# Windowed attention and MLP on one core: masks as a bias in PSUM for row 0, a shared normalisation, and a different order of loads

## The chip, the cores and the metric

One core of a Trainium2 chip. The metric is the device time of one execution in microseconds (us), and times are medians over several executions. With one core there is no second die to compare with, but every execution carries its mean granted TensorE clock.

## The reference

```python
# q, k, v: (8, 8, 576, 64); w_in: (512, 2048); w_out: (2048, 512)
rel = pos[:, None] - pos[None, :]
mask_plain = (rel >= 0) & (rel < 32)                            # heads 0-3, "sliding"
mask_dil = (rel >= 0) & (rel < 128) & (rel % 4 == 0)            # heads 4-7, "dilated"
attn = softmax(where(mask, scale * q @ k.T, -1e9)) @ v          # per batch row and head
x = attn.transpose(0, 2, 1, 3).reshape(8 * 576, 512)
out = relu(x @ w_in) ** 2 @ w_out
```

(Softmax and MLP are shortened to one line each.) The kernel works by batch row, 0 to 7. The MLP of one row runs on TensorE while the attention of the next is prepared. Only row 0 has no MLP to hide behind, and the change is about row 0, plus one load in row 1.

## The kernel before

The parts touched, with cuts marked. Row 0 in program order; each engine executes its own instructions in this order.

```python
    def load_sliding_v(b):                        # v as fp32 into a staging tile
        vv = v[b, 0:HH].rearrange("h (m p) d -> p h m d", p=QB)
        if b == 0:
            for m in range(NB):                   # six transfers, one for each 96 tokens
                nc.sync.dma_start(out=sv[PADP:P, :, m, :], in_=vv[:, :, m, :])
        else: ...
    def halo_sliding(b, mp):                      # rows that reach into the block before
        m0, m1 = max(1, 2 * mp), 2 * mp + 2
        nc.scalar.copy(vp[b % 2][0:PADP, m0:m1, :, 0:D],
                       vp[b % 2][P - PADP : P, m0 - 1 : m1 - 1, :, 0:D])
    def fill_gen(): ...                           # filler: 2 matmuls of 512 columns, result unused
    def softmax(u, ps, mask):
        nc.scalar.activation(AT[:, u, 0:UW], ps[:, :, 0 : UW // 2], ACTF.Exp, scale=scale)
        nc.vector.tensor_mul(AT[:, u, 0:UW], AT[:, u, 0:UW], mask)
    def s_sliding(b, hp):
        tiles = [pa(f"ps{b}_{hp}_{half}") for half in range(2)]   # two PSUM tiles of two banks
        ...                                       # scores, start=True
        for half, ps in enumerate(tiles):
            softmax(2 * hp + half, ps, maskp)
    def normalize(b, what, pav, w):               # value product / sum of weights
        ...
        nc.vector.reciprocal(rcp[0:w], pv[:, :, :, D])
        nc.vector.tensor_tensor(out=x[0:w], in0=pv[:, :, :, 0:D], in1=rcp..., op=ALU.mult)
        return x
...
    load_sliding_v(0)
    load_dilated_v(0, nc.sync)
    cast_sliding_v(0, (0, 2))                     # fp32 -> fp16 on GpSimd
    load_w_in()                                   # three pieces, also issued by GpSimd
    cast_sliding_v(0, (4,))
    cast_dilated_v(0)
    for hp in range(2):
        t_sliding(0, n, hp, False)                # transposes of q and k
    pending.append(fill_gen())
    for hp in range(2):
        s_sliding(0, hp)
        pump(1)                                   # one filler round
    halo_sliding(0, 0)
    for a in range(2):
        t_dilated(0, m, a, False)
    halo_sliding(0, 1)
    pump(1)
    xs = [av_sliding(0, 0)]                       # first value product
    pump(1)
    for g in range(2):
        s_dilated(0, g)
        pump(1)
    halo_sliding(0, 2)
    ...
    load_v(1)
    cast_sliding_v(1)
    load_w_out((3,))
    cast_dilated_v(1)
    ...
    for mp in (1, 2):
        xs.append(av_sliding(0, mp))
        pump(1)
    ...                                           # x_sliding and av_dilated, with fillers
    zs = [av_dilated(0, 1, 0)]
    begun = [mm1_begin(0, 0)]
    zs.append(av_dilated(0, 1, 1))
    begun.append(mm1_begin(0, 1))
    x_dilated(0, 0, ys, False)
    x_dilated(0, 1, zs, False)                    # then TensorE's unbroken stream
```

The softmax here doesn't subtract the row's maximum and nothing guards it: scores larger than these inputs give would overflow.

## Time and profile before

| what | before |
|---|---|
| time, median (range), 3 runs | 310.51 us (309.01 to 310.66) |
| span of the profiled execution | 307.3 us |
| TensorE busy | 290.7 us, 95% |
| q and k of row 0 have landed | 6.62 us |
| first exponential of sliding / dilated scores starts | 8.69 / 14.70 us |
| third value product starts | 17.86 us |
| third reciprocal of the dilated heads starts | 22.23 us |
| TensorE's unbroken stream starts | 25.06 us |
| first 60 matmuls of the stream take | 13.11 us |

How to read it: after 25 us TensorE is busy nearly without a break, so the end of the program is the start of that stream plus its length. Whatever shortens row 0's chain moves the end; all else in row 0 is free. The profile's lines are in the prediction below.

### The profile page before, as it was taken

To read this page: it belongs to the slowest core of one execution; us is meant where nothing else is said; L and a number is where in the kernel's file an instruction comes from. 1 tells how busy PE (TensorE), PEld (TensorE's weight loads), DVE (VectorE), ACT (ScalarE), POOL (GpSimd) and SP (SyncE) were. 2 spreads that over 40 slices of the span, in tenths; PEclk is the share of its full clock that TensorE was granted. 3 is DMA by queue.
4 is the path that set the end of the run, shared out by engine and by line. 5 is a ranking of instruction groups with operands and counts; after the bars stand their busy time and mean duration, and the time that the engine had idled before them with its cause. 6 is when DMAs were issued, how large, how long until landed. Compare 5 with 4: busy or idle time off the path is not lost.

```text
span 307.3 us, 7108 instructions
## 1 busy us (share of the span) xinstructions
PE 290.7 (95%) x2874; PEld 196.5 (64%) x2874; DVE 207.9 (68%) x433; ACT 183.4 (60%) x326; POOL 71.7 (23%) x114
## 2 busy tenths in 40 slices
PE   1798998999999999999999999999999999999994
PEld 1454554554455469656998997569756975785583
DVE  7784448568953798489748983898378934834652
ACT  2766648668645982598339834983499336425620
POOL 4481008413805303400630083007000000000000
PEclk9999999999999999999999999999999999999999
DMA  7899997999699999999968996889500020003004
GB/s 116 188 200 213 206 171 114 189 241 205 112 214 194 222 199 185 240 154 191 171 130 188 181 184 97 219 166 186 165 10 2 0 109 29 0 4 136 2 0 137
DMA packets 67024, 43.58 MB, mean 142 GB/s; under 512 B 48624, under 2 KB 59376, under 8 KB 66992
## 3 DMA queue, kind: packets, MB, share of 16 engines
q1 hardware_dynamic: 57920, 28.45, 44.9%
q0 software_dynamic: 9072, 14.68, 27.7%
q8 instruction: 22, 0.36, 0.5%
q14 instruction: 10, 0.08, 0.1%
HBM read 36.70 MB, written 16.52 MB: 173 GB/s over the span
## 4 chain that ended last, share of the span: by engine, by line
PE 71%; ACT 10%; DVE 7%; DMA 6%; issue 2%; SPq 2%; POOL 1%; POOLq 0%; DVEq 0%
PE ph L294 27%; PE pa L371 16%; PE pb L371 8%; PE po L437 7%; ACT AT L547 5%; DMA ns<-in_q_dram 5%; PE pc L371 4%; ACT rt L317 3%; PE paw L619 3%; PE pav L605 2%; PE px L634 1%; PE py L652 1%; DVE AT L548 1%; DMA QKTp<-dp 1%; PE pf L491 1%
## 5 line engine op out<-in xcount | busy, mean ns | idle before, releaser
L294 PE MATMUL ph<-xT,wi 128*128 128x512 f16 (+1 forms) x640 | 133.4, 359 | 0.7 <-ACT xT L658 0.7
L317 ACT ACTIVATE rt<-ph 128x512 f16<-128x512 f32 x144 | 84.9, 603 | 33.5 <-PE ph L294 33.5
L294 PEld LDWEIGHTS <-wi 128*128 128x128 f16 x640 | 68.6, 114 | 46.8 <-issue 0.8
L318 DVE TENSOR_TENSOR g<-rt 128x512 f16<-128x512 f16 x144 | 62.2, 435 | 42.7 <-ACT rt L317 41.1
L371 PEld LDWEIGHTS <-g 128*128 128x128 f16 x448 | 42.5, 98 | 5.3
L170 POOL CAST vp<-sv 128x512 f16<-128x512 f32 x24 | 17.5, 760 | 108.6 <-DMA sv<-in_v_dram 62.1
L371 PEld LDWEIGHTS <-gs 128*128 128x128 f16 x336 | 31.6, 98 | 3.7 <-DVE gs L328 0.3
L437 PE MATMUL po<-wo,g 128*128 128x512 f16 x128 | 33.1, 379 | 0.0
L398 DVE TENSOR_TENSOR ov<-pb,ov 128x512 f32<-128x512 f32 x14 | 9.7, 691 | 29.9 <-PE pb L371 18.2
L371 PE MATMUL pa<-wt,gs 128*128 128x256 f16 x224 | 28.5, 273 | 0.0
L371 PE MATMUL pb<-wt,g 128*128 128x256 f16 x224 | 27.7, 273 | 0.0
L178 POOL CAST vd<-sd 128x512 f16<-128x512 f32 (+1 forms) x32 | 24.2, 782 | 3.1 <-DMA sd<-in_v_dram 2.4
L387 ACT COPY ov<-pa 128x512 f32<-128x512 f32 x14 | 8.2, 585 | 26.8 <-PE pa L371 26.8
L591 DVE TENSOR_TENSOR x_d<-paw,rcp_d 72x512 f16<-72x512 f32 x32 | 22.0, 687 | 1.1
L547 ACT ACTIVATE AT<-pz 128x576 f16<-128x576 f32 x32 | 20.0, 712 | 1.7 <-PE pz L576 1.6
L548 DVE TENSOR_TENSOR AT<-AT,maskp 128x576 f16<-128x576 f16 x32 | 17.3, 545 | 5.1 <-ACT AT L547 2.6
L547 ACT ACTIVATE AT<-ps 128x576 f16<-128x576 f32 x32 | 19.2, 662 | 1.2 <-PE ps L557 0.9
L658 ACT COPY xT<-py 128x576 f16<-128x576 f16 x16 | 10.2, 640 | 14.7 <-PE py L652 14.6
L591 DVE TENSOR_TENSOR x_p<-pav,rcp_p 96x512 f16<-96x512 f32 x24 | 16.5, 687 | 0.8
L387 ACT COPY ou<-pa 128x512 f32<-128x512 f32 x14 | 8.2, 588 | 14.5 <-PE pa L371 14.5
L548 DVE TENSOR_TENSOR AT<-AT,maskd 128x576 f16<-128x576 f16 x32 | 14.9, 484 | 2.6 <-ACT AT L547 0.6
L640 ACT COPY xT<-px 128x576 f16<-128x576 f16 x16 | 10.2, 638 | 9.2 <-PE px L634 8.6
(81 smaller groups left out, 306.6 us busy)
## 6 DMA issues: line engine op xcount, KB each, us to landing
sv<-in_v_dram SPq DMA_DIRECT2D x14, 288.0 KB, 6.2
dp<-nr SPq DMA_DIRECT2D x12, 288.0 KB, 4.1
out_dram<-ou SPq DMA_DIRECT2D x6, 512.0 KB, 3.1
out_dram<-ov SPq DMA_DIRECT2D x6, 512.0 KB, 3.5
sd<-in_v_dram SPq DMA_DIRECT2D x8, 320.0 KB, 7.3
ns<-in_k_dram POOLq DMA_DIRECT2D x8, 288.0 KB, 5.2
ns<-in_q_dram POOLq DMA_DIRECT2D x8, 288.0 KB, 6.4
sd<-in_v_dram SPq DMA_DIRECT2D x8, 256.0 KB, 6.7
```

The source lines that it names most:

```text
L170: nc.gpsimd.tensor_copy(vp[b % 2][:, m : m + 2, :, 0:D], sv[:, :, m : m + 2, :].rearrange("p h m d -> p m h d"))
L178: nc.gpsimd.tensor_copy(vd[b % 2][p0:P, t, c : c + 2, :, 0:D], sd[p0:P, t, :, D * c : D * (c + 2)].rearrange("p h (c d) -> p c h d", d=D),)
L294: nc.tensor.matmul(ph[:, t0:t1], wi4[ffc // 4][:, dmk, :, ffc % 4], xT[:, dmk, x0 : x0 + t1 - t0], start=(dmk == 0 and t0 == 0), stop=(dmk ...
L317: nc.scalar.activation(rt, ph[:], ACTF.Relu)
L318: nc.vector.tensor_mul(g[:, ffc, :], rt, rt)
L371: nc.tensor.matmul(banks[bank][:, t], a(k, t), b(k), start=(new and t == 0 and k == 0), stop=(k == HF - 1), skip_group_check=True,)
L387: nc.scalar.copy(ot, banks[A])
L437: nc.tensor.matmul(po, g[:, ffc, t * P : (t + 1) * P], wo[ffc // 4][:, ffc % 4, :], start=(ffc == 0), stop=(ffc == NFF - 1),)
L547: nc.scalar.activation(AT[:, u, 0:UW], ps[:, :, 0 : UW // 2], ACTF.Exp, scale=scale)
L548: nc.vector.tensor_mul(AT[:, u, 0:UW], AT[:, u, 0:UW], mask)
L591: nc.vector.tensor_tensor(out=x[0:w], in0=pv[:, :, :, 0:D], in1=rcp[0:w].unsqueeze(3).to_broadcast([w, 2, HH, D]), op=ALU.mult,)
L640: nc.scalar.copy(xT[:, 0:2, t0 : t0 + 288], px[:, 0:UW].rearrange("x (c t) -> x c t", c=2),)
```

## The change

Its intent, as far as the code tells: take VectorE out of row 0's chain. The masks are no longer multiplied in after the exponential; a bias of 0 or -30000 is put into the score tile by an identity matmul first, and the scores accumulate onto it. Sliding v comes in two transfers, so that SyncE issues less. GpSimd's casts stand between the pieces of w_in. Two of the dilated normalisations give half of their work to ScalarE. The sliding halo copies go to VectorE. Row 0's order is new: the first dilated scores come ahead of the first value product. Row 1: w_out's last quarter is issued ahead of the casts of v.

```diff
 def load_sliding_v(b):
-    if b == 0:
-        for m in range(NB):
-            nc.sync.dma_start(out=sv[PADP:P, :, m, :], in_=vv[:, :, m, :])
-    else: ...
+    for h in (0, 2):
+        nc.sync.dma_start(out=sv[PADP:P, h : h + 2], in_=vv[:, h : h + 2])
 def halo_sliding(b, mp):
-    nc.scalar.copy(
+    copy(nc.scalar if b else nc.vector,
+for o, m in ((biasp, maskp), (biasd, maskd)):
+    nc.vector.tensor_scalar(out=o, in0=m[:, 0 : UW // 2], scalar1=-1.0, scalar2=30000.0,
+                            op0=ALU.add, op1=ALU.mult)
 def softmax(u, ps, mask):
-    nc.vector.tensor_mul(AT[:, u, 0:UW], AT[:, u, 0:UW], mask)
+    if mask is not None: ...                      # row 0 has none
+def biased(b, ps, bias):
+    if b == 0:
+        for e in range(2):
+            nc.tensor.matmul(ps[:, e, 0 : UW // 2], ident, bias, start=True, stop=False, ...)
+    return ps
 def s_sliding(b, hp):                             # s_dilated likewise
-    tiles = [pa(f"ps{b}_{hp}_{half}") for half in range(2)]
+    tiles = [biased(b, pa(f"ps{b}_{hp}_{half}"), biasp) for half in range(2)]
 def normalize(b, what, pav, w, shared=False):     # shared: row 0, second dilated half
+    if shared:
+        for h in range(HH):
+            nc.scalar.activation(x[0:w, 1, h], pv[:, 1, h, 0:D], ACTF.Copy,
+                                 scale=rcp[0:w, 1, h : h + 1])
+    n = 1 if shared else 2                        # VectorE: n of 2 halves
 def x_dilated(b, t, xs, wide):                    # row 0, t = 1: copy split likewise
+        nc.scalar.copy(o[:, 0], i[:, 0])
+        nc.vector.tensor_copy(o[:, 1], i[:, 1])
 ...                                               # row 0
-    cast_sliding_v(0, (0, 2)); load_w_in(); cast_sliding_v(0, (4,)); cast_dilated_v(0)
+    cast_sliding_v(0, (0,)); load_w_in(0); cast_sliding_v(0, (2, 4))
+    cast_dilated_v(0, (0,)); load_w_in(1); cast_dilated_v(0, (1,)); load_w_in(2)
     for hp in range(2):
         s_sliding(0, hp)
-        pump(1)
-    halo_sliding(0, 0)
     for a in range(2):
         t_dilated(0, m, a, False)
-    halo_sliding(0, 1)
     pump(1)
+    s_dilated(0, 0)
+    pump(1)
+    halo_sliding(0, 0)
     xs = [av_sliding(0, 0)]
     pump(1)
-    for g in range(2):
-        s_dilated(0, g)
-        pump(1)
-    halo_sliding(0, 2)
+    s_dilated(0, 1)
+    pump(1)
+    halo_sliding(0, 1)
 ...
-    cast_sliding_v(1)
+    nc.gpsimd.tensor_copy(seen, sv[:, 3, NB - 1, 0:1])   # row 1's sliding v has landed
     load_w_out((3,))
-    cast_dilated_v(1)
+    cast_v(1)
 ...
     for mp in (1, 2):
         xs.append(av_sliding(0, mp))
+        if mp == 1:
+            halo_sliding(0, 2)
         pump(1)
```

(x_dilated(0, 0) and the second mm1_begin change places; the small copies that hold v back until q has landed move from VectorE to GpSimd.)

More of the change, by code (lines that the diff above doesn't have):

```diff
@@ L95 @@
     maskd = const.tile([P, UW], FP16, name="maskd")
+    biasp = const.tile([P, UW // 2], FP16, name="biasp")
+    biasd = const.tile([P, UW // 2], FP16, name="biasd")
     def load_qk(b):
@@ L125, in load_sliding_v @@
         vv = v[b, 0:HH].rearrange("h (m p) d -> p h m d", p=QB)
-        if b == 0:
-            for m in range(NB):
-                nc.sync.dma_start(out=sv[PADP:P, :, m, :], in_=vv[:, :, m, :])
-        else:
-            for h in (0, 2):
-                nc.sync.dma_start(out=sv[PADP:P, h : h + 2], in_=vv[:, h : h + 2])
+        for h in (0, 2):
+            nc.sync.dma_start(out=sv[PADP:P, h : h + 2], in_=vv[:, h : h + 2])
     def load_dilated_v(b, eng):
@@ L142, in load_v, with load_w_in @@
         load_dilated_v(b, nc.sync)
-    def load_w_in():
-        f0 = 0
-        for t, w in zip(wi, wi_cols):
-            nc.gpsimd.dma_start(
-                out=t, in_=moe_w_in[:, f0 : f0 + w].rearrange("(dh dl) f -> dl dh f", dl=P)
-            )
-            f0 += w
+    def load_w_in(n):
+        f0, w = sum(wi_cols[:n]), wi_cols[n]
+        nc.gpsimd.dma_start(
+            out=wi[n], in_=moe_w_in[:, f0 : f0 + w].rearrange("(dh dl) f -> dl dh f", dl=P)
+        )
     def load_w_out(gs):
@@ L172, in cast_sliding_v, with cast_dilated_v @@
             )
-    def cast_dilated_v(b):
-        for t in range(2):
+    def cast_dilated_v(b, ts=(0, 1)):
+        for t in ts:
             p0 = 64 * t
@@ L184, in halo_sliding @@
         m0, m1 = max(1, 2 * mp), 2 * mp + 2
-        nc.scalar.copy(
-            vp[b % 2][0:PADP, m0:m1, :, 0:D], vp[b % 2][P - PADP : P, m0 - 1 : m1 - 1, :, 0:D]
+        copy(
+            nc.scalar if b else nc.vector,
+            vp[b % 2][0:PADP, m0:m1, :, 0:D],
+            vp[b % 2][P - PADP : P, m0 - 1 : m1 - 1, :, 0:D],
         )
@@ L271 @@
             hi_[:, 0:w].unsqueeze(1).to_broadcast([P, m.shape[1], w]),
+        )
+    for o, m in ((biasp, maskp), (biasd, maskd)):
+        nc.vector.tensor_scalar(
+            out=o, in0=m[:, 0 : UW // 2], scalar1=-1.0, scalar2=30000.0, op0=ALU.add, op1=ALU.mult
         )
@@ L547, in softmax @@
         nc.scalar.activation(AT[:, u, 0:UW], ps[:, :, 0 : UW // 2], ACTF.Exp, scale=scale)
-        nc.vector.tensor_mul(AT[:, u, 0:UW], AT[:, u, 0:UW], mask)
+        if mask is not None:
+            nc.vector.tensor_mul(AT[:, u, 0:UW], AT[:, u, 0:UW], mask)
+    def biased(b, ps, bias):
+        if b == 0:
+            for e in range(2):
+                nc.tensor.matmul(
+                    ps[:, e, 0 : UW // 2], ident, bias, start=True, stop=False, skip_group_check=True
+                )
+        return ps
     def s_sliding(b, hp):
-        tiles = [pa(f"ps{b}_{hp}_{half}") for half in range(2)]
+        tiles = [biased(b, pa(f"ps{b}_{hp}_{half}"), biasp) for half in range(2)]
         for half, ps in enumerate(tiles):
@@ L560, in s_sliding @@
                         QKTp[b % 2][r, 0, hp, PADP + QB * m : PADP + QB * (m + 1)],
-                        start=True,
+                        start=b > 0,
                         stop=True,
+                        skip_group_check=b == 0,
                     )
         for half, ps in enumerate(tiles):
-            softmax(2 * hp + half, ps, maskp)
+            softmax(2 * hp + half, ps, maskp if b else None)
     def s_dilated(b, g):
-        tiles = [pa(f"pz{b}_{g}_{h}") for h in range(2)]
+        tiles = [biased(b, pa(f"pz{b}_{g}_{h}"), biasd) for h in range(2)]
         for h, ps in enumerate(tiles):
@@ L579, in s_dilated, with normalize @@
                             QKTd[b % 2][r, 0, a, q0 : q0 + QD],
-                            start=True,
+                            start=b > 0,
                             stop=True,
+                            skip_group_check=b == 0,
                         )
         for h, ps in enumerate(tiles):
-            softmax(4 + 2 * g + h, ps, maskd)
-    def normalize(b, what, pav, w):
+            softmax(4 + 2 * g + h, ps, maskd if b else None)
+    def normalize(b, what, pav, w, shared=False):
         x = xp.tile([QB, 2, HH, D], FP16, name=f"x{b}_{what}", tag="x")
@@ L590, in normalize @@
         nc.vector.reciprocal(rcp[0:w], pv[:, :, :, D])
+        if shared:
+            for h in range(HH):
+                nc.scalar.activation(
+                    x[0:w, 1, h], pv[:, 1, h, 0:D], ACTF.Copy, scale=rcp[0:w, 1, h : h + 1]
+                )
+        n = 1 if shared else 2
         nc.vector.tensor_tensor(
-            out=x[0:w],
-            in0=pv[:, :, :, 0:D],
-            in1=rcp[0:w].unsqueeze(3).to_broadcast([w, 2, HH, D]),
+            out=x[0:w, 0:n],
+            in0=pv[:, 0:n, :, 0:D],
+            in1=rcp[0:w, 0:n].unsqueeze(3).to_broadcast([w, n, HH, D]),
             op=ALU.mult,
@@ L625, in av_dilated @@
                 )
-        return normalize(b, f"d{t}_{a}", pav, QD)
+        return normalize(b, f"d{t}_{a}", pav, QD, b == 0 and t == 1)
     def x_sliding(b, half, xs, wide):
@@ L657, in x_dilated @@
         t0 = (b * S + 288 * t) % XW
-        nc.scalar.copy(
-            xT[:, 2:4, t0 : t0 + 288].rearrange("x c (i r) -> x c i r", r=DIL),
-            py[:, 0:UW].rearrange("x (c r i) -> x c i r", c=2, r=DIL),
-        )
+        o = xT[:, 2:4, t0 : t0 + 288].rearrange("x c (i r) -> x c i r", r=DIL)
+        i = py[:, 0:UW].rearrange("x (c r i) -> x c i r", c=2, r=DIL)
+        if b == 0 and t == 1:
+            nc.scalar.copy(o[:, 0], i[:, 0])
+            nc.vector.tensor_copy(o[:, 1], i[:, 1])
+        else:
+            nc.scalar.copy(o, i)
     def attn_scores(b, gap, less=0, hooks={}):
@@ L706 @@
     n, m = nsd[0]
-    nc.vector.tensor_copy(sv[64:P, 0, :, 0], n[0:64, 0, 0:NB])
+    nc.gpsimd.tensor_copy(sv[PADP:64, :, 0, 0], n[PADP:64, :, 0])
     load_sliding_v(0)
-    nc.vector.tensor_copy(sd[64:P, :, 0, 0], n[0:64, 0, 0:2])
+    nc.gpsimd.tensor_copy(sd[64:P, :, 0, 0], n[64:P, 0, 0:2])
     load_dilated_v(0, nc.sync)
-    cast_sliding_v(0, (0, 2))
-    load_w_in()
-    cast_sliding_v(0, (4,))
-    cast_dilated_v(0)
+    cast_sliding_v(0, (0,))
+    load_w_in(0)
+    cast_sliding_v(0, (2, 4))
+    cast_dilated_v(0, (0,))
+    load_w_in(1)
+    cast_dilated_v(0, (1,))
+    load_w_in(2)
     for hp in range(2):
@@ L759 @@
     zs.append(av_dilated(0, 1, 1))
+    x_dilated(0, 0, ys, False)
     begun.append(mm1_begin(0, 1))
-    x_dilated(0, 0, ys, False)
     x_dilated(0, 1, zs, False)
```

## The prediction

> **What bounds the kernel now.** I read the page first (engine shares, slices), then a table by stage, then the chain in order of time for the first 30 us, then the timeline of each engine there, then the waits after 25 us.
>
> ```profile
> PE 290.7 (95%) x2874; PEld 196.5 (64%) x2874; DVE 207.9 (68%) x433; ACT 183.4 (60%) x326; POOL 71.7 (23%) x114
> 20.00:25.00 5.00, 3.58 (x54) 2.31 (x53) 3.38 (x8) 1.90 (x3) 3.76 (x7) 1.00 1.15 212
> 25.00:38.00 13.00, 12.94 (x60) 6.76 (x60) 6.02 (x15) 8.86 (x16) 0.54 (x2) 1.00 1.11 209
> 100.00:307.00 207.00, 202.28 (x1971) 149.38 (x1969) 141.54 (x284) 120.94 (x220) 32.44 (x48) 1.00 0.60 123
> ```
>
> The first line is the page; the others are stages (window, its length, busy time and count of PE, PEld, DVE, ACT, POOL, then clock, DMA share, GB/s). From 25 us on TensorE is 97 to 99% busy: only what moves the moment at which its unbroken stream starts, or a wait inside the stream, can move the end. The change touches row 0's attention, which is all of the first 25 us, so its worth is the shift of that moment. The chain in order of time (start, length, what) shows how it is reached:
>
> ```profile
> 16.13 1.20 ACT AT L547 x2
> 17.35 0.77 DVE AT L548
> 18.28 0.70 DVE x_p L591
> ...
> 22.45 0.69 DVE x_d L591
> 23.29 0.70 DVE x_d L591
> 24.03 0.32 PE py L652 x4
> 24.37 0.65 ACT xT L658
> 25.06 13.11 PE ph L294 x60
> ```
>
> From the last mask product at 17.35 to 23.98 it is VectorE with its six normalisations and short round trips to TensorE; then four transposes, one ScalarE copy, and the stream. Upstream, from the timelines:
>
> ```profile
> 8.82 1.04 PE L491 MATMUL pf<-maskp,ident 128*128 128x512 f16 x2
> 10.38 0.61 PE L491 MATMUL pf<-maskp,ident 128*128 128x512 f16 x2
> 16.04 2.09 DVE L548 TENSOR_TENSOR AT<-AT,maskd 128x576 f16<-128x576 f16 x3 [0.20 <-ACT AT L547]
> 17.21 2.63 POOL L178 CAST vd<-sd 128x512 f16<-128x512 f32 x4 [0.81 <-DMA sd<-in_v_dram]
> 7.34 3.96 SPq L128 DMA_DIRECT2D sv<-in_v_dram  x6
> 12.89 2.31 POOL L147 DMA_DIRECT2D wi<-in_moe_w_in_dram  x3
> ```
>
> Six v issues take 3.96 us of SyncE; the third sliding cast waits until 15.78, the dilated ones until 17.21. In the stream itself one wait is of interest, from the list of waits between 40 and 110 us:
>
> ```profile
> PE ps L557 <- DMA QKTp<-dp: 0.5, 1, 0.5
> ```
>
> It stands at 71.5 us (0.64 us beyond the matmul's own columns) and ends a chain of transfers for row 2.
>
> **What the Trainium skill says.** (1) "VectorE: DVE Perf Modes", The perf-mode tier table: a two-input 16-bit product from SBUF runs at 2x, anything from PSUM in fp32 at 1x. The trace agrees: the 576-wide mask product takes 0.46 us undisturbed, a 512-wide normalisation from PSUM 0.69. (2) "SBUF — State Buffer", Who interferes with whom: a VectorE instruction with two SBUF inputs contends with a GpSimd one that reads SBUF. It agrees: the same product takes 0.86 us at 11.48 and 0.77 at 17.35, both beside a GpSimd cast. (3) "ScalarE: Activation LUTs", What ACT_TABLE_LOAD costs: an activation costs 186 ns + 0.833 ns per element, a per-partition scale adds 93 ns, neighbours overlap by 93 ns. The first half agrees (666 ns for 576 wide; the exponentials take 650); the kernel before has no per-partition scale, so that part is untested. (4) "TensorE: Matmul & The Clock Gate", What's actually happening: half clock until some 3.4 us of activity. It agrees: the two filler matmuls at 8.9 us need 0.97 us on the chain, those at 10.4 need 0.43, and the clock record turns at 10.3.
>
> **The change part by part.** I replay row 0 in the new program order with durations of this trace.
>
> Fence and v load: the small copies that hold v back leave VectorE (where they stood behind the masks until 7.38) for GpSimd, free when q lands at 6.62. v issues at about 6.9 instead of 7.34, in two pieces instead of six. But until 9.5 us the engines are full with q and k, and the whole sliding v (590 KB) then needs about 2.8 us at 200 to 227 GB/s, so it lands near 12.3; the first cast now needs all of it: 12.9 instead of 12.03. Third cast 14.9 (was 16.39), dilated v cast by 16.1 and 18.1 (were 18.60 and 19.84). w_in's first piece is issued near 12.9 as before; being alone it lands near 18.5 (20.0 before), the others 1 to 2 us earlier. None of this is on the chain above: w_in is first needed at 21.4, and its last piece has some 3.5 us to spare.
>
> Bias, sliding: 16 identity matmuls of 288 columns, in groups of four. The first four start when the transposes end (7.65) at half clock: 4 x 0.24 = 0.96 us, against a wait for the q/k copies that ended at 8.23. So scores start near 8.65, 0.4 us late, exponentials near 9.1 (8.69 before). The second four wait for the score tiles that the exponentials free (9.75 and 10.3); those exponentials end near 12.1 instead of 11.45. The mask products (0.46 + 0.86 at the end) disappear; they ended at 12.34. Gain on this leg: about 0.2 us.
>
> Dilated q/k: ScalarE no longer stops for the first halo (12.06 to 12.46), VectorE is free at 11.3. Ready near 13.4 instead of 13.80.
>
> Middle: now the dilated scores of the first group come first. Exponential 13.85 to 14.5; the first value product needs that tile's bank, so its normalisation ends near 15.9 instead of 14.95; the second group's bias needs the bank which that frees: scores 16.2, exponentials 16.6 to 17.8 (before: 16.13 to 17.32, then masks to 18.13). Second value product 17.3, normalised at 18.64 (18.96 before). Then a step that was not there: the last sliding halo now queues on VectorE behind that normalisation, about 0.25 us, so the third value product starts near 18.95 instead of 17.86.
>
> Tail: from the third value product to the second dilated one TensorE does 0.25 + 4 fillers of 0.43 + two transposes of 0.26 + 0.25 = 2.7 us in order, so it is at 21.7 instead of 20.93, and its normalisation ends at 23.1 instead of 22.30. Sharing: four 64-wide ScalarE scalings at about 0.21 (0.165 fixed + 0.053 + 0.093 - 0.10, an estimate from the ScalarE page and this trace) make 0.94 us against 0.69 for VectorE's whole one; two in a row are 1.8 us of ScalarE, then the first copy 0.55, then half a copy 0.40: 2.7 us from the third reciprocal, against 2.59 measured before (22.42 to 25.01). Sharing is even. The stream starts between 25.5 and 26.1, 0.4 to 1.0 us LATER.
>
> w_out's last quarter: issued when row 1's sliding v has landed (45.2) instead of after its casts (47.01). The DMA engines stood idle from 46.8 to 48.7, so it lands nearly 2 us earlier, and row 2's loads behind it (landing at 54.6 to 59.2) about 1 us earlier; the wait of 0.64 us at 71.5 goes. Sum: +0.7 - 0.6 = about 0, from a before whose three runs lie at 309.0, 310.5 and 310.7 (mean 310.1).
>
> I then lean 0.4 us to the fast side, as my replay puts late several steps that hang on a bank coming free, and whoever arranged the order presumably saw a gain: 309.7.
>
> **Rivals.** (a) VectorE was the true limit and is relieved: eight products (4.96 us of VectorE in row 0), half of two normalisations and two fence copies go. For it: VectorE is busy nearly without a break from 15.4 to 20. Then the stream starts near 23.5 and the time is about 308.3. Against it: the two-tile ring of score banks sets the order of the middle. (b) Latency takes the place of throughput, as in my replay, with no relief at 71.5: 311. (c) The clock stays at half longer: two filler rounds at 8.8 and 10.4 are gone, and only 16 x 288 columns come in; cold dilated transposes would cost 1 us more: 311 to 312. (d) The transfers hide everything: the stream's loads have 3 us or more to spare, so even a start 2 us earlier would not meet them.
>
> **Range and chances.** Start of the stream -1.6 to +1.6 us, relief at 71.5 0 to -0.6, the spread between runs about 0.8 either way: 307.6 to 311.6. A move of 2% is 6.2 us, a quarter of all that precedes the stream; faster by that much 0.02, slower 0.01, within 0.97.
>
> **What would show it.** Right: the first bias matmuls near 7.7 us at about 0.24 us each; no mask product in row 0; first dilated exponential near 13.8; the third value product waiting for the VectorE halo and starting after 18.5; ScalarE's small scalings at 0.2 us apiece ending last before the copies; w_in's first piece landing before 19; no wait for the transposed q/k near 71 us; stream start 25 to 26.2. Wrong: a stream that starts before 24.5 (rival a), cold fillers after 11 us (rival c), or a new wait inside the stream for w_in, w_out or row 1's v.

## More of the kernel before

One line more for later, the row "TensorE's granted clock in tenths" of the page of the kernel before, in 40 slices. (The clock's record begins where it first turns to full, here at 10.30 us, so the half clock before that doesn't show in the row.)

```profile
PEclk9999999999999999999999999999999999999999
```

## The result, and the profile after

| | before | after |
|---|---|---|
| time, median (range), 4 runs each | 310.59 us (309.01 to 311.16) | 315.18 us (315.05 to 315.32) |
| span of the profiled execution | 307.3 us | 313.5 us |
| q and k landed | 6.62 | 7.14 |
| third sliding / first dilated exponential starts | 10.26 / 14.70 | 12.09 / 15.52 |
| third value product starts | 17.86 | 20.92 |
| third reciprocal of the dilated heads starts | 22.23 | 24.98 |
| stream starts | 25.06 | 29.06 |
| first 60 matmuls of the stream take | 13.11 | 15.89 |

The kernel after takes 1.56% longer: ratio 1.0156, 95% interval 1.0119 to 1.0193. A ratio is the mean time of one kernel's fast runs over that of the other's of the same rounds, so it is not quite the ratio of the medians quoted. That is within the 2% that the prediction put at 0.97, but the time lies 5.5 us above its number and well above its range.

The page of the kernel after: VectorE has the work taken from it that the change meant to take (207.9 to 202.6 us), and TensorE is busy *longer*; the row of its clock says why in part.

```profile
PE 296.2 (94%) x2886; PEld 198.9 (63%) x2886; DVE 202.6 (65%) x429; ACT 183.7 (59%) x331; POOL 70.5 (22%) x117
...
PEclk9997799999999999999999999999999999999999
```

The table by stage of the kernel after (columns as in the prediction: window, length, busy time of PE, PEld, DVE, ACT, POOL, clock, DMA share, GB/s) has the same two stages that were shown of before. From 25 to 38 us TensorE did 55 matmuls in place of 60 and the clock stood at 0.74:

```profile
20.00:25.00 5.00, 3.87 (x54) 2.44 (x54) 3.44 (x9) 2.00 (x4) 4.18 (x8) 1.00 1.11 182
25.00:38.00 13.00, 10.77 (x55) 4.80 (x56) 4.29 (x13) 6.94 (x17) 0.34 (x2) 0.74 1.12 208
```

The chain in order of time of the kernel after (start, length, what), cut to its three delays (pieces named "issue", of 0.05 us at most, are left out too):

```profile
8.35 1.07 PE ps L556 x4
9.42 0.37 PE ps L568 x5
9.82 0.66 ACT AT L549
10.52 1.18 PE ps L556 x4
11.70 0.60 PE ps L568 x12
12.29 2.02 PE pd L539 x18
...
20.48 0.39 DVE vp L162
20.92 0.43 PE pav L624 x8
...
25.21 0.93 ACT x_d L606 x4
26.16 0.42 DVE x_d L610
26.58 0.12 DVE rcp_d L603
26.73 0.93 ACT x_d L606 x4
27.68 0.43 DVE x_d L610
28.15 0.44 PE py L671 x4
28.61 0.41 ACT xT L680
29.06 15.89 PE ph L296 x60
```

First block: the bias matmuls (L556) and the 18 dilated transposes (L539) stand on the chain one after the other, both rounds of bias at half clock (the clock record turns full at 14.17 us; before, at 10.30). Second: the third value product waits for a halo copy on VectorE. Third: from the third reciprocal (24.98) to the stream it takes 4.1 us, before 2.8, because ScalarE's four small scalings and VectorE's half of the same normalisation run **in turn**, not side by side. VectorE's own timeline of the kernel after says it outright (in brackets: idle time before, and what ended it):

```profile
26.16 0.42 DVE L610 TENSOR_TENSOR x_d<-paw,rcp_d 72x256 f16<-72x256 f32 x1 [0.98 <-ACT x_d L606]
...
27.68 0.42 DVE L610 TENSOR_TENSOR x_d<-paw,rcp_d 72x256 f16<-72x256 f32 x1 [0.98 <-ACT x_d L606]
29.04 0.46 DVE L681 COPY xT<-py 128x288 f16<-128x288 f16 x1 [0.95 <-ACT xT L680]
```

The last line is the split copy: its two halves ran in turn as well.

Inside the stream, the list of TensorE's waits from 40 to 110 us of the kernel after no longer has a wait for the transposed q and k (QKTp), as predicted:

```profile
PE pav L624 <- ACT vp L160: 0.5, 1, 0.5
PE pz L588 <- ACT AT L549: 0.2, 1, 0.2
PE pav L624 <- DVE rcp_p L603: 0.2, 1, 0.2
```

So the span's 6.2 us are: stream start +4.0, its first 60 matmuls +2.8, the wait at row 2 -0.6. The difference of the medians is smaller (4.6) mainly because the profiled execution of before is a quick one (309.11 us against a median of 310.59), while that of after lies near its median (315.32 against 315.18). It has two spells of half clock in the stream and the other three runs of after have one each, yet all four lie within 0.27 us; what makes up for the second spell isn't known.

### The profile page after: what moved, and what is told of

Read it like the earlier page. It is cut to its first block, busy times and chain, and to the rows that moved or that the text cites.

```text
span 313.5 us, 7131 instructions
## 1 busy us (share of the span) xinstructions
PE 296.2 (94%) x2886; PEld 198.9 (63%) x2886; DVE 202.6 (65%) x429; ACT 183.7 (59%) x331; POOL 70.5 (22%) x117
## 4 chain that ended last, share of the span: by engine, by line
PE 76%; ACT 12%; DVE 6%; issue 3%; DMA 2%; POOL 0%; DVEq 0%; POOLq 0%
PE ph L296 30%; PE pa L373 15%; PE pb L373 8%; PE po L439 7%; ACT AT L549 7%; PE pc L373 4%; ACT rt L319 4%; PE paw L638 3%; PE pav L624 2%; DVE AT L551 2%; DMA ns<-in_q_dram 2%; PE py L671 1%; PE px L653 1%; DVE g L320 1%; PE pd L539 1%
## 5 line engine op out<-in xcount | busy, mean ns | idle before, releaser
L296 PE MATMUL ph<-xT,wi 128*128 128x512 f16 (+1 forms) x640 | 136.2, 364 | 0.5 <-ACT xT L680 0.5
L320 DVE TENSOR_TENSOR g<-rt 128x512 f16<-128x512 f16 x144 | 61.5, 430 | 44.9 <-ACT rt L319 43.6
L373 PEld LDWEIGHTS <-g 128*128 128x128 f16 x448 | 42.5, 98 | 5.3
L610 DVE TENSOR_TENSOR x_d<-paw,rcp_d 72x512 f16<-72x512 f32 (+1 forms) x32 | 21.4, 670 | 3.0 <-ACT x_d L606 2.0
L174 POOL CAST vd<-sd 128x512 f16<-128x512 f32 (+1 forms) x32 | 22.7, 736 | 0.6 <-DMA sd<-in_v_dram 0.2
L683 ACT COPY xT<-py 128x576 f16<-128x576 f16 x15 | 9.6, 641 | 12.3 <-PE py L671 12.3
L551 DVE TENSOR_TENSOR AT<-AT,maskp 128x576 f16<-128x576 f16 x28 | 13.6, 487 | 3.9 <-ACT AT L549 1.6
L439 PEld LDWEIGHTS <-g 128*128 128x128 f16 x128 | 10.3, 98 | 8.3 <-DVE g L320 0.3
```

The source lines that it names most:

```text
L174: nc.gpsimd.tensor_copy(vd[b % 2][p0:P, t, c : c + 2, :, 0:D], sd[p0:P, t, :, D * c : D * (c + 2)].rearrange("p h (c d) -> p c h d", d=D),)
L296: nc.tensor.matmul(ph[:, t0:t1], wi4[ffc // 4][:, dmk, :, ffc % 4], xT[:, dmk, x0 : x0 + t1 - t0], start=(dmk == 0 and t0 == 0), stop=(dmk ...
L320: nc.vector.tensor_mul(g[:, ffc, :], rt, rt)
L373: nc.tensor.matmul(banks[bank][:, t], a(k, t), b(k), start=(new and t == 0 and k == 0), stop=(k == HF - 1), skip_group_check=True,)
L439: nc.tensor.matmul(po, g[:, ffc, t * P : (t + 1) * P], wo[ffc // 4][:, ffc % 4, :], start=(ffc == 0), stop=(ffc == NFF - 1),)
L610: nc.vector.tensor_tensor(out=x[0:w, 0:n], in0=pv[:, 0:n, :, 0:D], in1=rcp[0:w, 0:n].unsqueeze(3).to_broadcast([w, n, HH, D]), op=ALU.mult,)
```

## The experiments

Eighteen kernels were run; the kernel before ran along on the same chip. Where the text compares traces it takes "stream minus q", the time from q's landing to the start of the stream, because q lands anywhere from 6.5 to 7.7 us in any of the kernels: 18.4 us before, 21.9 after. Two runs with row 0 as before and its tail untouched (b_wout 17.5) or filled (e_tail 18.5) show that this number too carries about 1 us of noise. A ratio is always against the kernel before. Waits of TensorE in the text count from the end of the columns of the matmul before; the lists of waits model a later end and give 0.1 to 0.2 us less.

**Spells of half clock.** In all 20 traces each stretch at half clock that lies between two at full clock is 3.41 us long or twice that. So an execution's mean granted clock tells how many such windows it had: one takes 0.5 x 3.41 / 310 = 0.0055 off the mean. 15 of 55 runs of the kernel before had a mean below 0.996; those average 311.98 us (311.84 without the one that is slow), the other 40 310.22. So a spell costs about 1.7 us, which is also half of 3.41, and the kernel before has one in a quarter of its executions. The counts for the others stand with each experiment.

### The four direct suspects

`a_unshared` (the kernel after, both shared steps undone):

```diff
-        return normalize(b, f"d{t}_{a}", pav, QD, b == 0 and t == 1)
+        return normalize(b, f"d{t}_{a}", pav, QD)
-        if b == 0 and t == 1:                     # split copy of xT
+        if False:
```

> The changed kernel without the sharing: row 0's normalisations and its last copy are whole again, on one engine each. Theory S (sharing serialises: in the changed kernel's trace VectorE's half waits 0.98 us for ScalarE's four scalings, twice, and the second half copy waits for the first): from the third dilated reciprocal to the stream 2.6 us as in the kernel before instead of 3.9, so the stream starts about 1.2 us earlier; if the busier tail also keeps TensorE's clock up, 1.7 to 3.4 us more. In all 311 to 314 us against 315.2. Rival (sharing is even, the loss is upstream in the bias and the order): 315 us within 0.3.

Measured: 313.25 us (311.97 to 314.32), ratio 1.0081 [1.0040, 1.0121]. From the third reciprocal to the stream 2.8 us again, the profiled run without a spell, 2 of 6 runs with one. About half of the loss hangs on the sharing (ratio 1.0081 in place of 1.0156), through the chain and through the clock.

`b_share` (the kernel before with the sharing and the split copy alone).

> The kernel before with the sharing alone added. Theory S: the stream starts about 1.2 us later (26.3), time +1.2 us; +3 to +4.6 if the longer quiet tail also drops the clock. Rival (sharing is even): within 0.3 us of the kernel before.

Measured: 311.82 us (311.14 to 313.79), ratio 1.0048 [1.0007, 1.0088]. The third reciprocal comes at 22.63, the stream at 26.59: 3.96 us, where before has 2.83. The same wait, on VectorE's timeline of this run, and the table by stage with half clock at the start of the stream:

```profile
23.80 0.42 DVE L597 TENSOR_TENSOR x_d<-paw,rcp_d 72x256 f16<-72x256 f32 x1 [0.98 <-ACT x_d L593]
...
25.32 0.42 DVE L597 TENSOR_TENSOR x_d<-paw,rcp_d 72x256 f16<-72x256 f32 x1 [0.98 <-ACT x_d L593]
```

```profile
25.00:38.00 13.00, 11.60 (x48) 5.51 (x49) 5.13 (x12) 7.79 (x15) 0.49 (x2) 0.87 1.11 210
```

5 of 6 runs had a spell. The sharing alone is therefore slower, though it moves work off the busy engine: both engines read the same PSUM tile, and in the built program VectorE's half waits on ScalarE's semaphore. Builds, without a run on the chip, tell what orders them: with an output tile for each engine the wait stays, with a tile of reciprocals for each it stays, and with a PSUM tile for each it is gone. So it is the read of the PSUM tile that is ordered. The Trainium skill, "PSUM — Partial Sum Buffer", PSUM bank collisions raise a hardware error, says that two engines on one bank must be kept apart, but that accesses to different banks run clean. The two halves lie in different banks of one tile, so by that page the order isn't needed; two PSUM tiles would be the way to get rid of it. That was not run. The split copy waits likewise (VectorE 0.83 us for ScalarE in this run), but its tile is a single bank, 1024 fp16 elements per partition, so there the order is needed.

`a_warm` (the kernel after, nine filler matmuls around the last transposes):

```diff
     begun.append(mm1_begin(0, 1))
+    pw = pa("pwarm")
+    for _ in range(6):
+        nc.tensor.matmul(pw[:, 0], ident, maskp[:, 0:TOKC], start=True, stop=True)
     x_dilated(0, 1, zs, False)
+    for _ in range(3):
+        nc.tensor.matmul(pw[:, 1], ident, maskp[:, 0:TOKC], start=True, stop=True)
```

> The changed kernel with nine filler matmuls in the tail of row 0, where TensorE idles, and nothing else. Theory C (a quiet stretch in the tail lowers TensorE's clock to half for the start of the stream): the clock record no longer drops after the stream starts, its first 60 matmuls take 13.1 us instead of 15.9, and the time falls by 1.7 to 3.4 us to 312 to 313.5, with the stream starting where it did within 0.3 us. Rival (the drop is an accident of the one profiled run): no change, 315 us.

Measured: 313.34 us (312.62 to 315.52), ratio 1.0096 [1.0051, 1.0142]. No run had a spell (all at 0.997 or above). In the profiled run the stream starts at 29.55, later than after's, yet the last of its first 60 matmuls starts at 42.56 in place of 44.57. They take 13.39 us, where before has 13.11: at full clock TensorE waits for VectorE's half of the split copy, which runs from 29.53 to 30.00. Part of the gain is given back: a wait of 0.94 us for QKTp that ends at 77.11 and one of 1.04, for a value product, that ends at 118.0. These six runs, with no spell in them, show what the chain alone costs: about 3 us.

`a_halo` (the kernel after, last sliding halo earlier):

```diff
     halo_sliding(0, 1)
+    halo_sliding(0, 2)
 ...
         xs.append(av_sliding(0, mp))
-        if mp == 1:
-            halo_sliding(0, 2)
```

> The changed kernel with row 0's last sliding halo moved ahead of the second sliding normalisation on VectorE. Theory H (the third value product waited for it): that product starts at about 19.7 instead of 20.9 us, the stream about 1.1 us earlier, the time 313.5 to 314.3. Rival (the tail is bound by VectorE and ScalarE alone): the stream moves less than 0.3 us.

Measured: 313.18 us (312.51 to 314.60), ratio 1.0087 [1.0048, 1.0127], one spell in 6 of 6 runs. The third value product starts 12.7 us after q lands in place of 13.8, the stream 20.7 in place of 21.9. The late halo was worth 1.1 us of the chain.

### The other parts alone

Each of these is the kernel before with one part of the diff. All five parts put together give the kernel after statement for statement.

`b_bias` (bias and no mask products, old order):

> The kernel before with the masks as a bias in row 0 and nothing else. Theory B (the bias matmuls run at half clock on the path and cost about what the mask products gave): first exponential 0.5 to 0.7 us later, third 1.0 to 1.4 us later, stream within 0.6 us of the kernel before at the same clock state, time within 0.6 us. Rival V (VectorE was the bound, so the products' 5 us of it come back): stream 1 us or more earlier. Rival W (late by the full delay of the exponentials): stream 1.2 us later.

311.68 us (310.73 to 312.75), ratio 1.0032 [0.9987, 1.0077]: no gain, though eight products of VectorE are gone. Third exponential 4.7 us after q (before 3.6).

`b_order` (the new order and the halos on VectorE, masks still multiplied):

> The kernel before with the changed order of row 0 (dilated scores ahead of the first value product, fewer fillers early, sliding halos on VectorE) and nothing else; masks still as products. Theory O (the order makes one long chain through two score tiles and the last halo): third value product 2 us later, stream 1.5 to 2.5 us later, time +1.5 to +2.5 us. Rival (the order is neutral, the loss belongs to bias and sharing): stream within 0.5 us.

315.38 us (314.41 to 315.71), ratio 1.0151 [1.0103, 1.0199]: alone it costs as much as the whole change. VectorE still has its mask products, and now the halos queue behind them; TensorE's value products wait for three halos, 2.5 us in sum. 4 of 6 runs had spells.

`b_loads` (v in two transfers, casts between w_in's pieces):

> The kernel before with only the loading of v in two transfers behind GpSimd's copies, and GpSimd's casts between the pieces of w_in. Theory L (hidden): v is issued 0.3 to 0.5 us earlier, the first cast ends 0.9 to 1.9 us later and holds up the first value product, yet VectorE has slack there; stream 0 to +0.8 us, w_in's last piece 1 to 2 us later, still before its use near 31 us; time within 0.8 us. Rival: the earlier end of the casts (1.7 us) brings the stream forward by 0.5 us or more.

311.79 us (311.09 to 313.25), ratio 1.0043 [0.9997, 1.0088]. The first value product waits for GpSimd's first cast of v. Since in the old order ScalarE's halo copy stands ahead of its copies of the dilated q and k, the first dilated exponential starts at 17.45 in place of 14.70.

`b_wout` (w_out's last quarter ahead of row 1's casts):

> The kernel before with only w_out's last quarter issued ahead of row 1's casts. Theory D (row 2's chain of transfers ends in a wait of 0.64 us near 71.5 us, and the quarter's earlier landing shortens that chain): the quarter lands about 1.7 us earlier, the wait goes, stream start unchanged, time -0.4 to -0.8 us. Rival (the chain is held elsewhere): the wait stays, 0.

311.29 us (309.52 to 313.02), ratio 1.0025 [0.9973, 1.0076]. The quarter lands at 52.13 as before: the move gains nothing, since row 1's v landed only at 46.5 and the issue waits for that. Row 2's wait for QKTp stays (0.82 us). And TensorE has a new wait of 1.7 us from 52.7 us on, for a normalisation in row 1, behind a mask product that took 2.80 us in place of 0.46 beside GpSimd's casts. This reappears below.

### The parts against each other

`c_noorder` (everything but the order):

> The changed kernel with row 0's old order: old places of the value products, all eleven filler rounds, sliding halos on ScalarE; bias, sharing, loading and w_out's move stay. Theory O (the order is the largest loss, as the order alone cost 4.5 us and the other four parts 0.4 to 1.0 us each): 311.5 to 313 us, 2 to 3.5 us below the changed kernel. Rival (the parts only lose together, the order costs nothing beside the bias): 315 us.

317.82 us (315.90 to 319.09), ratio 1.0228 [1.0190, 1.0265], the slowest of all. Sliding v lands at 15.70 and the first value product waits 2.5 us for its cast. So the new order, which is bad by itself, hides the late v: the parts don't add up, and the shares of a single-part table must not be summed.

`c_haloact` (the kernel after, halos back on ScalarE, the last one early):

> The changed kernel with row 0's sliding halos back on ScalarE, the last one ahead of the second value product as in a_halo; the order of scores and values stays. Theory H2 (VectorE's halos are late because they queue and contend with GpSimd's casts): 0.3 to 0.8 us below a_halo's 313.2, the second value product up to 0.3 us earlier. Rival (ScalarE is as late with them, behind the exponentials): equal to a_halo or 0.5 us above.

315.78 us (313.12 to 317.42), ratio 1.0150 [1.0103, 1.0197]: no better. A halo now queues behind exponentials, and the value products wait for halos 1.8 us in sum. Its pair is `a_halo`, which differs in the engine alone and has a ratio of 1.0087: so the runs give no sign that VectorE was the wrong engine for them; what `a_halo` shows is that the last one stood too far back in its queue. (In the trace of c_haloact the clock also turned full late, at 16.15 us.)

`c_warm` (the kernel before, 44 filler matmuls of 128 columns right at the start, four in the tail) and `c_warm_bias` (the same with the bias):

```diff
     nsd = {0: load_qk(0)}
+    wz = const.tile([P, P], FP16, name="wz")
+    nc.vector.memset(wz, 0.5)
+    pz_ = pmool.tile([P, TOKC], FP32, name="pwz", tag="pm")
+    for _ in range(44):
+        nc.tensor.matmul(pz_[:, 0:P], wz, wz, start=True, stop=True)
```

> The kernel before with 44 filler matmuls of 128 columns on TensorE while it waits for q and k, and four fillers in the tail. Theory C (TensorE's clock is at half until some windows of activity have passed, and a quiet window in the tail lowers it again in some runs): clock full by 8.5 us instead of 10.3 or later, stream 0.3 to 0.7 us earlier, no dip in any run, so the slow ones of the kernel before (311.4 and above) vanish: 308.8 to 309.8 us, narrow. Rival (the fillers delay q's transposes, or the clock is not on the path): 310 us or above.

> c_warm with the masks as a bias. Theory BC (the bias loses only because its matmuls run at half clock): at full clock each takes 0.12 instead of 0.24 us, the exponentials come within 0.3 us of c_warm's, and the missing mask products bring the stream forward by 0.3 to 1 us: 0.3 to 1 us below c_warm. Rival (bias waits for banks, not for the clock): equal to c_warm or up to 1 us above.

Measured: 310.95 us (308.98 to 311.94), ratio 1.0003 [0.9964, 1.0041], and 311.34 us (310.20 to 312.08), ratio 1.0019 [0.9984, 1.0054]. Third exponential 2.9 us after q lands with masks, 3.8 with the bias, both with the clock full from 6.0 and 6.6 us on (c_warm's fell back once, from 9.41 to 12.83). So about 0.9 us of the bias's cost has nothing to do with the clock: the bias of *both* tiles is issued before the scores of the first, and so those scores wait for the second tile's bank. c_warm's earlier exponentials didn't reach the stream: the first dilated one came no earlier (8.2 us after q, before 8.1), and a mask product then fell beside a cast and took 1.76 us.

### Undoing causes in the kernel after

These four and the next two were run to settle how much each cause holds in the presence of the others.

`d_inter` (the kernel after, bias tile by tile):

```diff
-        tiles = [biased(b, pa(f"ps{b}_{hp}_{half}"), biasp) for half in range(2)]
+        tiles = [pa(f"ps{b}_{hp}_{half}") for half in range(2)]
         for half, ps in enumerate(tiles):
+            biased(b, ps, biasp)
```

> The changed kernel with each tile's bias issued just ahead of that tile's own scores, not both tiles' ahead of both. Theory T (the first tile waits for the second one's bank): the third exponential comes 0.4 to 0.7 us sooner after the first, the seventh 0.7 to 1.1 us sooner after the fifth; second value product and stream 0.7 to 1.2 us earlier; time 313.5 to 314.6 against 315.2. Rival (the clock sets it): under 0.3 us.

315.54 us (314.24 to 316.43), ratio 1.0159 [1.0117, 1.0202]. The exponentials are earlier (third: 4.1 us after q in place of 4.95; first dilated one: 7.3 in place of 8.4), but the second and third value products then wait 1.7 us for the halos in place of 1.0. The gain on the third is real and hidden; of the 1.1 us on the dilated one a part is the clock, which turned full at 11.92 in this run and at 14.17 in the kernel after.

`d_six` (the kernel after, v in six transfers):

> The changed kernel with row 0's v in six transfers again. Theory L2 (within the new order the first value product waits for a bank, not for v): first cast 1.5 to 3 us earlier, first value product and stream within 0.4 us, time 314.6 to 315.5. Rival (v is on the path here too, as it is with the old order): 1 us or more below the changed kernel.

315.65 us (314.08 to 317.39), ratio 1.0174 [1.0124, 1.0224]: no effect, as the halos set this leg as well (1.5 us of TensorE's idle time ahead of the third product). GpSimd's first cast starts at 11.41 in place of 13.96.

`d_early` (the kernel after with the 44 early fillers):

> The changed kernel with 44 filler matmuls of 128 columns while TensorE waits for q and k. Theory C2 (half clock until 14 us costs the bias matmuls 0.5 us and the dilated transposes 0.9 us): clock full before 9 us, fifth exponential 1 to 1.6 us sooner after q has landed, stream as much earlier, 313.3 to 314.3 us. Rival (an early quiet window drops it again, or banks and v hold the chain): within 0.5 us of 315.2.

314.59 us (313.28 to 315.95), ratio 1.0132 [1.0088, 1.0176]. The clock is full at 4.01 but falls back at 7.42, 17.66 and 31.32, one window of 3.41 us each. Early fillers alone don't keep it.

`d_best` (the kernel after, unshared, halo early, bias tile by tile, early fillers, 1 + 3 tail fillers):

> The changed kernel with all four mended: bias tile by tile, last halo early, no sharing, fillers early and in the tail. If the mechanisms add up: third value product 10.0 to 10.8 us after q has landed (11.2 in the kernel before, 13.8 in the changed one), stream 17.2 to 18.2 us after q (18.4 before), no dip of the clock after it: 308.5 to 310 us, at or below the kernel before. Rival (v's late first cast, which stays, holds the first value product): 310.5 to 312.

312.47 us (310.77 to 314.47), ratio 1.0068 [1.0023, 1.0113]. More than half of the loss is gone. In the profiled run the clock fell twice (8.68 and 18.92), and the first value product waits 1.1 us for the cast of v, the second piece of which lands at 15.63.

`e_best6` (d_best with v in six transfers):

> This is the kernel after with all repairs at once: bias tile by tile, last sliding halo early, no sharing, early and tail fillers, and v in six transfers again. Theory T (the repairs leave only the longer chain of the new order, in which the first value product comes after the first dilated scores): the first value product no longer waits for v's first cast (1.13 us of TensorE's idle time in the same kernel with v in two), the stream starts 20.3 to 20.9 us after q lands (21.6 with v in two, 18.4 in the kernel before, 21.9 in the kernel after) and its first 60 matmuls stay under 13.3 us; time 311.3 to 312.0, ratio 1.002 to 1.006: still no better than before. Rival (v in two costs nothing in this order, as the run of six transfers alone suggests): stream at 21.4 to 21.8 after q, time 312.3 to 312.8 as with v in two. Second rival (all of the loss was in the repaired parts): stream at 18.4 to 19.0 after q, ratio 0.995 to 1.000.

311.97 us (310.17 to 313.19), ratio 1.0033 [0.9995, 1.0072]. Row 0 did what the second rival expected, and my theory of a longer chain in the new order fell: the stream starts at 24.31, 17.3 us after q, at least as early as with row 0 as before (17.5 to 18.5). The clock was full without a break from 6.29 us, the third exponential came 3.1 us after q and the first value product 7.3 (d_best: 3.6 and 9.4). One trace can't say how much of that is v and how much the clock, which in d_best fell. The table by stage of this run:

```profile
20.00:25.00 5.00, 4.40 (x54) 2.55 (x53) 2.67 (x7) 1.92 (x4) 5.00 (x10) 1.00 1.01 148
25.00:38.00 13.00, 13.00 (x62) 6.82 (x61) 6.38 (x15) 9.33 (x16) 0.95 (x4) 1.00 1.13 210
```

Yet the time is no better than before's, so the question is where the earlier start went. TensorE's waits from 44 to 60 us of this run:

```profile
PE pav L635 <- DVE rcp_p L614: 2.1, 1, 2.1
PE pav L635 <- ACT vp L164: 0.5, 1, 0.5
PE pz L599 <- ACT AT L558: 0.2, 1, 0.2
```

The first of these isn't there in the kernel before. The timelines of VectorE and of GpSimd show what stands behind it, two mask products in 3.78 us beside GpSimd's casts:

```profile
46.29 1.00 DVE L560 TENSOR_TENSOR AT<-AT,maskp 128x576 f16<-128x576 f16 x2 [1.20 <-ACT AT L558]
47.63 3.78 DVE L560 TENSOR_TENSOR AT<-AT,maskp 128x576 f16<-128x576 f16 x2 [0.34 <-ACT AT L558]
...
48.25 1.73 POOL L170 CAST vp<-sv 128x512 f16<-128x512 f32 x3
49.91 2.75 POOL L178 CAST vd<-sd 128x512 f16<-128x512 f32 x4
```

Of the two, the second took 3.24 us (48.17 to 51.40), seven times its 0.46. It ends just after the one pause that GpSimd makes between two casts, at 51.1; in b_wout the product of 2.80 us ends after the pause at 50.5, and before, one of 1.58 us after the pause at 48.7. The part of the change that seems to set this up is w_out's move (b_wout, which has nothing else, shows the wait too; d_best, with the move, has a product of 2.38 us): it puts all seven casts in one row, where before three stand ahead of w_out's issue and four behind it. In the kernel after itself it does no harm (four products in 1.8 us), since there row 1 comes so late that the casts are over. After that wait the clock also fell, from 54.07 to 57.49. A kernel like e_best6 with w_out where it was is thus the next to try.

`e_tail` (the kernel before with the four tail fillers and nothing else):

> This is the kernel before with four filler matmuls in the tail of row 0's attention and nothing else. Theory T (a third of the executions of the kernel before lose one window of half clock of 3.41 us at the start of the stream, worth 1.9 us each; tail fillers prevent it): no run with a granted clock of 0.993 to 0.995, mean 309.8 to 310.3 against 310.5 to 310.7 for the kernel before, ratio 0.997 to 0.9995; the stream starts 18.4 to 18.8 us after q lands. Rival (the windows do not hang on how busy TensorE is in the tail): as many runs with 0.993 to 0.995 as the kernel before has, ratio 0.999 to 1.003.

309.88 us (309.39 to 311.00), ratio 0.9981 [0.9954, 1.0007]. No spell in 6 runs (lowest clock 0.997), against 4 of 11 of the kernel before; the stream starts at 25.05. By itself 0 of 6 against 4 of 11 could be chance, and so could the ratio.

## Why the prediction was wrong

It put the stream's start at 25.5 to 26.1; measured 29.06. Of the 3 us beyond the later bound, 0.5 is q landing later, which no part of the change does. The rest is two steps of the sum, and a third term that isn't in the sum at all.

**"Sharing is even"**: this is the step that failed. It reckoned 2.7 us from the end of the third reciprocal to the stream against 2.59 before, so +0.1, with VectorE's half beside ScalarE's. From that reciprocal's start it measured 4.08 us, before 2.83: +1.25. Of that, 0.12 is the clock (the last transposes take 0.44 us in place of 0.32); in the eight other traces with the sharing it is 3.96, so the sharing itself costs 1.1. The size of ScalarE's part was right: four scalings take 0.93 us against 0.94 predicted. One lasts 0.31, which is 0.09 over the predicted fixed and per-element parts (0.165 and 0.053), so the Trainium skill's extra cost of a per-partition scale, cited there as untested, agrees with this trace. What was wrong is that the two run in series (idle 0.98 us for ScalarE, twice). b_share shows it alone (3.96 us), a_unshared shows it gone (2.8). The split copy gained nothing either: ScalarE's half takes 0.40 us in place of 0.64 for the whole, but at full clock the stream then waits about as long for VectorE's half (a_warm).

**The second bias round and the dilated transposes at full clock.** The first bias round at half clock was foreseen, at 4 x 0.24 us, and took 1.07. But the replay let the clock turn as before, at about 10.3 us. It turned at 14.17; the second round took 1.18 us and the 18 transposes 2.09 (before 1.17). The first dilated exponential came 1.2 us later than the 13.85 + 0.5 it was put at. This is rival (c), there as an alternative of 1 us; it came true together with the rest. Removing two filler rounds and the empty time in which the change leaves TensorE are what differs; that the fillers' removal *is* the cause is argued and not shown, as early fillers (d_early) turned the clock on and lost it again. Nor is it shown how much of the late turn is the change's at all: among the traces whose row 0 begins just as before's, the one that the prediction read has the earliest turn (10.30; b_wout 10.91, e_tail 12.94, b_share 13.84), and those that begin just as after's have 14.17, 14.11 (a_halo), 15.16 (a_unshared) and 15.33 (a_warm). What a late turn costs in the new order is seen in these last four: full clock 7.0, 7.2, 8.1 and 8.8 us after q, first dilated exponential 8.4, 8.5, 8.9 and 9.2, so half a us for each. The replay took the turn of one execution for a property of the kernel. And 0.9 of the 1.3 us by which the bias delays the third exponential isn't the clock at all but the order of its issue (c_warm_bias, d_inter).

**The clock in the tail.** The stream's first 60 matmuls took 15.89 us in place of 13.11. No term of the sum and no rival had this. Spells at half clock in 15 of 55 runs of the kernel before, but in 5 of 6 of b_share, 4 of 4 of the kernel after, 6 of 6 of a_halo, d_inter, d_six, d_early and c_noorder each, 4 of 6 of c_haloact; in 2 of 6 of a_unshared; in none of a_warm and none of e_tail. With a serial sharing in the tail nearly every run has one; with fillers in the tail and nothing else changed, none has. The runs that have both tail and early fillers do show some (c_warm 3 of 6, d_best 4, e_best6 3; c_warm_bias none), but in their profiled executions these lie at 8 to 13, at 19 and at 54 us and not at the start of the stream. In all eight traces with the sharing and no tail fillers a spell begins within 1.6 us of the stream's start. So I take it as shown that a quiet tail brings the spell at the start of the stream; that every spell in the timed runs lay there can't be seen from their mean clock, and b_order has spells (4 of 6 runs) without the sharing, in its trace from 19 to 26 us, ahead of the stream. At some 1.7 us a spell and 1.25 spells a run (clocks 0.989, 0.993, 0.994, 0.994) against 0.27, this is 1.7 us of the 4.6 to 4.8; the chain's 3.5 less the 0.6 at row 2 is the other 2.9.

**The late halo**: right. "The third value product starts near 18.95" was 20.92, later by what the steps ahead of it were late (0.5 and 1.2) and by 0.3 more, half of it the halo itself (0.39 us, reckoned at 0.25), and its wait of 1.0 us for VectorE's copy is in the list of waits. Likewise right: the first bias matmuls, no mask product left in row 0, the scalings' pace. Wrong without effect: w_in's first piece landed at 19.94 (before 20.00), not near 18.5, since it is issued behind a first cast that starts at 13.96.

**"None of this is on the chain"**, of v: wrong for the kernel before. Its chain in order of time, in a part that the prediction didn't show, has v's first cast on it:

```profile
11.42 0.62 POOL vp L170
12.04 0.02 issue
12.06 0.40 ACT vp L185
12.46 0.64 ACT QKTd L164
```

The cast, which starts 0.16 us after the second piece of v lands (11.26), releases a halo copy on ScalarE, which stands ahead of the copies of q and k. b_loads and c_noorder show what a later v does in that order (the first dilated exponential at 17.45 and 19.30). In the kernel after the new order takes the halo out of the way, and d_six shows that v's two transfers cost nothing *there*. So the step was wrong and did no harm. v in two landed at 13.8 to 15.7 us over the runs, not at 12.3: the first cast needs the last byte of both transfers.

**The 0.6 us at row 2**: the right number for the wrong reason. I had row 2's loads come earlier. They come later: the last QKTp transfer lands at 76.94 (before 71.91). The wait is gone because TensorE gets there later still, at 78.3 (before 72.05). b_wout keeps the wait, and in a_warm, d_best and e_best6, where the stream is early or quick, it is back.

**The rival that VectorE was the limit** is refuted: five of its us less work in row 0 (b_bias) gave nothing. And the lean of 0.4 us to the fast side had no number behind it; what it assumed, that a replay puts steps too late, was the wrong way round.

**What stays open:** whether the bias pays at all in a row 0 that is otherwise as before with a full clock; how much of e_best6's early start is v and how much the clock; and whether e_best6 without w_out's move would beat the kernel before. No version run beats it beyond doubt; e_tail, at 0.2%, is the only candidate.

## What to carry to other kernels

Before work is split between two engines, look whether both halves read one PSUM tile: if the program orders them, the sum of both times stands on the path, not the longer one. A stage with little for TensorE to do was paid for twice here, once in waits and once in the clock, so a chain that gets quieter should be checked against the clock of the stage after it. And parts of such a change are to be tried together as well as alone: here one order cost 4.5 us alone and saved about 2 beside a late load (c_noorder 1.0228, after 1.0156), and a gain in row 0 of e_best6 was taken back by casts in row 1.

## What the Trainium skill lacked or had wrong

- "SBUF — State Buffer", Who interferes with whom: it says that a two-input VectorE instruction contends with GpSimd's reads and that, for the 2-port modes, the one that issues first holds the ports for one instruction. It doesn't say that a two-input product can be held by a whole *row* of GpSimd casts: one of 0.46 us took 3.24, 2.80 and 1.58 us and ended each time only after GpSimd paused.
- "TensorE: Matmul & The Clock Gate", What's actually happening: its table names at least one idle window as the way back to half clock. Here the clock fell for one or two windows of 3.41 us at the start of the stream though no gap in TensorE's work ahead of it was longer than about 1.4 us (busy 1.84 of 4 us from 25 to 29). Further on the page speaks of a clock that falls over short idle times, but nowhere of how busy a window must be.
- No page has what follows from "PSUM — Partial Sum Buffer" for programs whose waits are set by tile: two engines that read different banks of one PSUM tile were run in turn by the program that was built, 0.98 us of waiting each time.
- "ScalarE: Activation LUTs", What ACT_TABLE_LOAD costs: four scalings of 64 elements with a per-partition scale took 0.93 us; by its numbers alone 1.05 (an estimate: 4 x 332 ns less three overlaps of 93). The extra cost of the scale agrees (0.09 us); the fixed part was shorter here, 0.165 us, which is what made the prediction's 0.94.
